# A tuned FFT-and-MoE kernel: six transfers are asked for by GpSimd in place of SyncE

## The chip, the cores and the metric

The kernel runs on one core of a Trainium2 chip. The metric is the device time of one execution in microseconds (us), median of several runs. TensorE (PE in the profile; PEld is its weight load), VectorE (DVE), ScalarE (ACT), GpSimd (POOL) and SyncE (SP) each work through their own list of instructions in order. SP computes nothing here: it only asks for transfers. A transfer asked for by SP or by GpSimd is then carried by the same 16 DMA engines; the profile calls the queue of SP's transfers q1 and that of GpSimd's q0.

## The reference

`x` has 8 batches of 3008 rows of 256 numbers. A real FFT over the rows, a complex 256 x 256 product with a soft threshold of 0.01, and the inverse FFT give `y`; then a two-layer network with an ELU between its layers runs on all 24064 rows.

```python
X = np.fft.rfft(x, axis=1)
Yr = Xr @ w_r - Xi @ w_i + b_r
Yi = Xr @ w_i + Xi @ w_r + b_i
Yr = np.sign(Yr) * np.maximum(np.abs(Yr) - lam, 0.0)   # Yi alike
y = np.fft.irfft(Y, n=x.shape[1], axis=1)
h = y @ w_in
g = np.where(h > 0.0, h, np.exp(np.minimum(h, 0.0)) - 1.0)
out = g @ w_out
```

## The kernel before

**The network's loop.** The rows of all batches are cut into 47 blocks of 512. Each block takes 8 iterations of the main loop (L1313), one for each pair of 128-wide slices of the hidden layer: `front` multiplies into `hps` (L1115) and ScalarE takes the exponential, `elu` and `finish_elu` finish the ELU on GpSimd or VectorE, and two iterations later `back` adds the pair to the block's output sums `ps_o` (L1189). After its 8th pair a block is copied to `osb`, one half by VectorE and one by ScalarE (L1200), and stored by four transfers of 128 rows each (L1209); some of these are cut in two where they cross a stretch of the output. `osb` has two buffers, so a block's copies need the stores of the block two before it to have ended.

**The FFT's units.** Both transforms are done as matrix products in two stages, cut into small units. While the network works on one batch, units of the next are put between its iterations by hand: `plan` writes, for each of a batch's 47 iterations, which units go ahead of the network's products (`f0`) and which after them (`f1`). For batch 1 they stand in the list `mid` (L1224) from iteration 10 on. A unit X is the second stage of the forward transform. Units M multiply by the weights and apply the threshold on GpSimd (L314, L315), six pairs q = 0 to 5, each into a tile `Y`. Units B are the first stage of the inverse, one for each pair. Units Y (`n` in `mid` for batch 1) are the second stage and give `yT`, which `front` reads. Units A belong to the forward transform of batch 2.

**The path around the change.** When the second half of pair q is done, `turn_Y` (L433) lets SP move `Y` to `Yx` with the parts re-ordered: `by_part` (L424) issues four transfers of 64 KB, for s = 0 with c = 0 and c = 1, then for s = 1 with c = 0 and c = 1 (L428). c chooses the half of the 128 partitions that is written. Unit B(1, q) then multiplies (L448): two products for s = 0, which need both c of s = 0, and two for s = 1. Its result is copied to `Bz`, by ScalarE alone (L150) or, for q = 5, half by ScalarE (L456) and half by VectorE (L457), and for q = 2 to 5 each quarter of `Bz`'s 256 KB goes to the DRAM tile `DB` in a transfer of its own (L466). `load_Bs` (L479) reads `DB` back in another order as `Bs`; the first of four such loads is cut, for batch 1, into 80 rows that come from pairs 0 to 4 and 16 rows that come from pair 5. The first unit Y of batch 1, Y(1, 0), reads that first `Bs` (L612), and the network needs its `yT` from iteration 40 on, where block 5 crosses from batch 0 to batch 1.

**What SP's list holds there.** Output block 3 (rows 1536 to 2047 of batch 0) ends in iteration 33. So SP's list runs in this order: four `Yx` transfers of pair 5; the `DB` store of pair 3; the four stores of block 3; the `DB` stores of pairs 4 and 5; the two parts of the first `Bs`; a store of batch 2's `DA` (L221); the other three `Bs`. SP takes them strictly one after another, and each waits for its own data first. GpSimd's list holds, at the same place, the threshold of pair 5 and then the ELU's minimum (L1166) of much later iterations, since between them the ELU is finished on VectorE.

Of the kernel before, what the change touches and what calls it, by code (L numbers as in the profile page):

```python
# [20 lines left out]
N2 = 64  # L21
# [8 lines left out]
def kernel(  # L30
# [11 lines left out]
    nc = tc.nc  # L42
    P = nc.NUM_PARTITIONS

    B, S, D = x.shape
# [375 lines left out]
        for Y_, yb, ch in todo:  # L421
            nc.vector.scalar_tensor_tensor(Y_, yb, LAM, ch, ALU.add, ALU.min)

    def by_part(dst, of):  # L424

        for s in range(2):
            for c in range(2):
                nc.sync.dma_start(dst[c * N2 : c * N2 + N2, :, s, :], of(c, s))  # L428

    def turn_M3():  # L430
        by_part(M3x, lambda c, s: M3[c][s * N2 : s * N2 + N2])

    def turn_Y(b, q):  # L433
        Y = Y_of.pop((b, q))
        Yx_of[b, q] = Yx = wk4.tile([P, 2, 2, D], BF16, name="Yx", tag="Y")
        by_part(Yx, lambda c, s: Y[s * N2 : s * N2 + N2, :, c * D : c * D + D])

    def unit_B(b, v, alone=False, on_dve=False, all_dve=False):
        if (b, v // 2) not in Bz_of:
# [643 lines left out]
    def pieces(t, k):  # L1083

        out_, c = [], 0
        while c < k:
            b, r = divmod(t + c, S)
            e = min(k, c + S - r)
            out_.append((b, r, c, e))
            c = e  # L1090
        return out_
# [79 lines left out]
    def back(i, split):  # L1171
        blk, fp = divmod(i, NPAIR)
        bs = blk * TB
        gT = g_of.pop(i)
        nq = TB // P // 2
        if fp == 0:
            po_of[blk] = [
                psO.tile([P, 2, E], F32, name="ps_o", tag="outp") for _ in range(nq)
            ]
        po = po_of[blk]  # L1180
        last = i == n - 1
        order = [(q, s, j) for q in range(nq) for s in range(2) for j in range(2)]
        if i == 0:
            order.sort(key=lambda z: z[1])
        elif last:
            order.sort(key=lambda z: (z[0], z[2]))
        for q, s, j in order:
            ft, i_ = 2 * fp + s, 2 * q + j
            nc.tensor.matmul(  # L1189
                po[q][:, j, :], lhsT=gT[:, s, i_ * P : i_ * P + P],  # L1190
                rhs=w_out_r[:, ft, :], start=(ft == 0 and j == 0),
                stop=(ft == NFT - 1), skip_group_check=True,
            )
        if fp < NPAIR - 1:
            return
        osb = late2.tile([P, 4, E], F32, name="osb", tag="osb")
        for q in range(nq):
            copy = nc.vector.tensor_copy if (last and q) or (split and q == 0) else nc.scalar.copy
            if not (last and q):
                copy(osb[:, 2 * q : 2 * q + 2, :], po[q][:])  # L1200
            for i_ in range(2 * q, 2 * q + 2):
                if last and q:
                    copy(osb[:, i_, :], po[q][:, i_ % 2, :])
                for b, t, c0, c1 in pieces(bs + i_ * P, P):
                    ov = out[b * S : b * S + S, :].rearrange("(r w j) e -> w r j e", w=4, j=8)
                    while c0 < c1:
                        w, r0 = t // WT, t % WT // 8
                        k = min(c1 - c0, (w + 1) * WT - t)
                        (nc.scalar if last and i_ % 2 else nc.sync).dma_start(  # L1209
                            ov[w, r0 : r0 + k // 8], osb[c0 : c0 + k, i_, :]  # L1210
                        )
                        t, c0 = t + k, c0 + k
        del po_of[blk]
# [4 lines left out]
    def plan(b):  # L1218
# [38 lines left out]
        for t, u in enumerate(seq, lead):  # L1257
            if u is None:
                continue
            if b and n1 < B:  # L1260
                mode[t] = "act" if u in on_act or u[0] == "M" else "pool"
            if mode[t] == "act" and u[0] != "M":
                k = {"y": "Y"}.get(u[0], u[0])
                c = {"y": b, "A": n2}.get(u[0], n1)
                if c < B:
                    dve = (False, True) if k == "B" else (k != "X" or b < 3 and u[1] == 7,)
                    f0[t].append(put(k, c, u[1], False, *dve))
            elif u[0] == "y":
                f0[t].append(put("Y", b, u[1]))
            elif u[0] == "n":  # L1270
                f0[t].append(put("Y", n1, u[1]))
            elif u[0] == "A":
                if n2 < B:
                    f0[t].append(put("A", n2, u[1]))
            elif b == 0 and u == ("B", 5):
                f0[t].append(put("B", n1, 5, False, True))
            else:
                f0[t].append(put(u[0], n1, *u[1:]))
            if u[0] == "M" and u[2] == 1:
                f1[t].append((turn_Y, (n1, u[1])))  # L1280
            if u == ("B", 5):
                for w, k in enumerate((0, 2, 3, 4)):
                    f1[t + k].append((load_Bs, (n1, w, 0, 4 * K1 - 16 * (b == w == 0))))
            if u == ("A", 5) and n2 < B:
                for part in ((0, 8), (8, NS)):
                    f1[t] += [(load_Z, (n2, a, *part)) for a in range(3)]
# [26 lines left out]
    for i in range(n + LAG):  # L1313
        if i == FILL:
            few.close()
        if i == LAG:
            back(0, False)
# [21 lines left out]
        if i < n:  # L1339
            for f, a in f1[r]:  # L1340
                f(*a)
            split = i > LAG and (i - LAG) % NPAIR == NPAIR - 1
            if split:
                back(i - LAG, True)
            elu(i, *h, pooled, on_act)
            if PER <= i < PER + 4:
                three_weights(*divmod(i - PER, 2))
            if 1 <= i < 5:
                if i < 3:
                    scale_w_in(2, True, i - 1)  # L1350
                scale_w_in(3, False, (i - 1) // 2, (i - 1) % 2)
            if i == n - 2:
                early_h = front(n - 1, True, False)
            elif early_h:
                early_h = None
        else:
            split = False
        if i > LAG and not split:
            back(i - LAG, False)
# [30 lines left out]
```

## Time and profile before

| | us |
|---|---|
| median of 3 runs | 873.0 |
| lowest and highest of them | 871.7, 874.85 |
| the profiled execution: time on the device | 873.84 |
| its span in the trace | 872.1 |
| TensorE matmul busy (share of the span) | 861.3 (99%) |
| ScalarE busy | 715.2 (82%) |
| VectorE busy | 665.9 (76%) |
| GpSimd busy | 589.4 (68%) |

The span is the time from the first to the last instruction of the trace; 1.7 us of the profiled execution lie around it. Busy times do not count the asking for transfers. In a timeline row the first two numbers are the start and the duration in us, then come the engine (SPq is SP's queue), the line, the operation, what it writes and reads, how many were merged (x4), and in brackets the engine's idle time just before and what ended it.

### The profile page before, as it was taken

The numbers are of one execution on the slowest core, as the hardware profiler recorded it, in microseconds if no ns is written. First come the engines' busy times: TensorE is split into PE (matmuls) and PEld (weight loads), VectorE is DVE, ScalarE is ACT, GpSimd is POOL, SyncE is SP. The second block draws the span as 40 slices with busy tenths as digits, with TensorE's granted clock in tenths as the row PEclk, the third lists the DMA queues.
The fourth block names the chain that finished last, engine by engine and source line by source line (L and its number), as shares of the span: only waits on it lengthen the run. The fifth ranks groups of instructions, "written<-read, shape, count | busy, mean of one in ns | idle before, by whom it ended". The sixth has DMA issues, their size and how long they took to land.

```text
span 872.1 us, 18551 instructions
## 1 busy us (share of the span) xinstructions
PE 861.3 (99%) x6773; PEld 675.6 (77%) x6773; DVE 665.9 (76%) x1103; ACT 715.2 (82%) x1255; POOL 589.4 (68%) x860
## 2 busy tenths in 40 slices
PE   8999999999999999999999999999999999999997
PEld 6567677887788877877778887788777878787776
DVE  8889778697776876768866787777777687788775
ACT  7878888888978889798887988879887888876664
POOL 8671630898757986588856888459874697734664
PEclk9999999999999999999999999999999999999999
DMA  8796446542484225653365342653337313240111
GB/s 248 263 300 208 115 114 196 161 142 73 122 242 140 80 73 157 208 159 96 87 179 182 123 110 74 210 159 116 97 92 221 88 38 86 76 144 25 40 36 49
DMA packets 114205, 116.11 MB, mean 133 GB/s; under 512 B 11569, under 2 KB 104241, under 8 KB 110753
## 3 DMA queue, kind: packets, MB, share of 16 engines
q1 hardware_dynamic: 109376, 87.40, 35.2%
q0 software_dynamic: 4448, 27.26, 9.4%
q8 instruction: 53, 0.87, 0.4%
q14 instruction: 40, 0.32, 0.1%
q10 hardware_dynamic: 288, 0.26, 0.1%
HBM read 53.28 MB, written 48.23 MB: 116 GB/s over the span
## 4 chain that ended last, share of the span: by engine, by line
PE 94%; DMA 2%; DVE 1%; POOL 1%; ACT 1%; issue 1%; SPq 0%; DVEq 0%; POOLq 0%
PE ps_o L1189 39%; PE hps L1115 34%; PE mps L334 6%; PE xps L242 3%; PE yps L612 2%; PE mps L1115 2%; PE bps L448 2%; PE aps L194 2%; PE mps L292 2%; DMA xt<-in_x_dram 1%; DMA yb<-in_w_i_dram 0%; DMA Bs<-DB 0%; DMA DB<-Bz 0%; DVE gT L1156 0%; PE aps L186 0%
## 5 line engine op out<-in xcount | busy, mean ns | idle before, releaser
L1156 DVE SCALAR_TENSOR_TENSOR gT<-Et,hps 128x512 fp32r<-128x512 f32 x630 | 402.8, 682 | 137.3 <-POOL Et L1166 127.3
L1189 PE MATMUL ps_o<-w_out_r,gT 128*128 128x256 f32 x3008 | 477.3, 301 | 0.0
L1189 PEld LDWEIGHTS ps_o<-w_out_r,gT 128*128 128x128 f32 x3008 | 404.3, 189 | 48.0 <-DVE osb L1200 0.2
L1166 POOL TENSOR_SCALAR Et<-Et 128x512 f32<-128x512 f32 x482 | 287.4, 615 | 208.2 <-ACT Et L1127 206.7
L1115 PE MATMUL hps<-yT,w_in_s 128*128 128x512 bf16 (+7 forms) x1620 | 366.7, 353 | 0.3
L1127 ACT ACTIVATE Et<-hps 128x512 f32<-128x512 f32 x514 | 282.7, 609 | 41.7 <-PE hps L1115 38.6
L1115 PEld LDWEIGHTS <-w_in_s 128*128 128x128 bf16 x1728 | 144.1, 98 | 104.8 <-issue 13.2
L1125 ACT ACTIVATE Et<-hps 128x512 f32<-128x512 f32 x192 | 104.5, 597 | 42.0 <-PE hps L1115 41.6
L1130 ACT ACTIVATE Et<-Et 128x512 f32<-128x512 f32 x192 | 110.5, 632 | 0.0
L350 POOL TENSOR_TENSOR Y<-yb,clip 128x512 bf16<-128x512 f32 x72 | 92.7, 1287 | 6.0
L346 POOL TENSOR_TENSOR yb<-yb,bias_bc 128x256 f32<-128x256 f32 x72 | 53.2, 739 | 11.3 <-DVE yb L341 11.2
L150 ACT CAST XT<-xps 128x768 bf16<-128x768 f32 x57 | 45.8, 804 | 15.9 <-PE xps L242 15.7
L150 ACT CAST yT<-yps 128x752 bf16<-128x752 f32 x56 | 44.1, 787 | 14.4 <-PE yps L612 14.4
L341 DVE TENSOR_TENSOR yb<-mps,yb 128x512 f32<-128x512 f32 x72 | 49.8, 692 | 7.2
L1158 DVE SCALAR_TENSOR_TENSOR gT<-hps,Et 128x512 fp32r<-128x512 f32 x78 | 50.2, 685 | 3.3
L349 POOL TENSOR_SCALAR clip<-yb 128x512 f32<-128x512 f32 x72 | 44.1, 613 | 6.3
L150 ACT CAST A<-aps 128x1024 bf16<-128x1024 f32 x40 | 40.7, 1019 | 7.9 <-PE aps L194 4.9
L150 ACT CAST Bz<-bps 128x1024 bf16<-128x1024 f32 x41 | 41.6, 1014 | 5.3 <-PE bps L448 5.0
L340 DVE TENSOR_TENSOR yb<-mps,bias_bc 128x256 f32<-128x256 f32 x72 | 30.5, 423 | 17.5 <-PE mps L334 15.7
L334 PE MATMUL mps<-wcat_s,XT 128*128 128x256 bf16 x288 | 43.2, 273 | 0.0
L1200 DVE COPY osb<-ps_o 128x512 f32<-128x512 f32 x46 | 31.7, 689 | 5.4 <-PE ps_o L1189 3.4
L260 POOL TENSOR_TENSOR XS<-XT 128x512 bf16<-128x512 bf16 x30 | 34.1, 1157 | 2.4 <-ACT XT L150 1.4
(214 smaller groups left out, 670.1 us busy)
## 6 DMA issues: line engine op xcount, KB each, us to landing
xt<-in_x_dram POOLq DMA_DIRECT2D x21, 1024.0 KB, 5.5
out_dram<-osb SPq DMA_DIRECT2D x158, 128.0 KB
Bs<-DB SPq DMA_DIRECT2D x30, 384.0 KB
Yx<-Y SPq DMA_DIRECT2D x168, 64.0 KB
DA<-A SPq DMA_DIRECT2D x19, 512.0 KB
DB<-Bz SPq DMA_DIRECT2D x19, 512.0 KB
Z<-DA SPq DMA_DIRECT2D x21, 384.0 KB
xt<-in_x_dram POOLq DMA_DIRECT2D x6, 512.0 KB, 5.8
```

Of the source, the lines that this page charges most:

```text
L150: nc.scalar.copy(dst, src)
L334: nc.tensor.matmul(out_, lhsT=lhs[:, dt] if lhs is not None else sum_of(dt, ch)[:, oc : oc + P], rhs=w[:, dt, :], start=(dt == 0), stop=(d ...
L346: nc.gpsimd.tensor_tensor(yb[:, D : 2 * D], yb[:, D : 2 * D], bias_bc[:, D : 2 * D], ALU.add)
L350: nc.gpsimd.tensor_tensor(Y_of[b, q][:, i, :], yb[:], clip[:], ALU.subtract)
L1115: nc.tensor.matmul(hps[s][:, c0:c1], lhsT=w_in_s[:, dt, ft * P : ft * P + P], rhs=yT_of[b][:, dt, t0 : t0 + c1 - c0], start=(dt == 0), sto ...
L1125: nc.scalar.activation(Et[:, s], hps[s], AF.Relu, scale=-1.0)
L1127: nc.scalar.activation(Et[:, s], hps[s], AF.Exp)
L1130: nc.scalar.activation(Et[:, s], Et[:, s], AF.Exp, scale=-1.0)
L1156: nc.vector.scalar_tensor_tensor(o, e, -1.0, h, ALU.add, ALU.max)
L1158: nc.vector.scalar_tensor_tensor(o, h, 0.0, e, ALU.max, ALU.add)
L1166: nc.gpsimd.tensor_scalar(e, e, 1.0, 0.0, ALU.min, ALU.max)
L1189: nc.tensor.matmul(po[q][:, j, :], lhsT=gT[:, s, i_ * P : i_ * P + P], rhs=w_out_r[:, ft, :], start=(ft == 0 and j == 0), stop=(ft == NFT ...
```

## The change

In `turn_Y` of batch 1's last pair, q = 5, the transfers with c = 1 (for s = 0 and for s = 1) are issued by GpSimd and those with c = 0 by SP as before. The four stores of output block 3 are issued by GpSimd. Nothing else differs: PE, DVE and ACT have the same instructions in the same order. SP's list loses six transfers and keeps the order of the others. In GpSimd's list the six stand behind the last threshold of pair 5 and ahead of the next minimum of the ELU: the two `Yx` pieces, then the four stores.

```diff
-    def by_part(dst, of):
+    def by_part(dst, of, shared=False):
 
         for s in range(2):
             for c in range(2):
-                nc.sync.dma_start(dst[c * N2 : c * N2 + N2, :, s, :], of(c, s))
+                eng = nc.gpsimd if shared and c else nc.sync
+                eng.dma_start(dst[c * N2 : c * N2 + N2, :, s, :], of(c, s))
...
-        by_part(Yx, lambda c, s: Y[s * N2 : s * N2 + N2, :, c * D : c * D + D])
+        by_part(
+            Yx, lambda c, s: Y[s * N2 : s * N2 + N2, :, c * D : c * D + D], (b, q) == (1, 5)
+        )
...
-                        (nc.scalar if last and i_ % 2 else nc.sync).dma_start(
+                        eng = nc.scalar if last and i_ % 2 else nc.sync
+                        (nc.gpsimd if blk == 3 else eng).dma_start(
                             ov[w, r0 : r0 + k // 8], osb[c0 : c0 + k, i_, :]
                         )
```

## The prediction

> **What bounds the kernel now.** I read the page's busy times first, then the chain of work that ended last, then what TensorE waited for.
>
> ```profile
> span 872.1 us, 18551 instructions
> PE 861.3 (99%) x6773; PEld 675.6 (77%) x6773; DVE 665.9 (76%) x1103; ACT 715.2 (82%) x1255; POOL 589.4 (68%) x860
> PE 94%; DMA 2%; DVE 1%; POOL 1%; ACT 1%; issue 1%; SPq 0%; DVEq 0%; POOLq 0%
> ```
>
> TensorE is busy in 861.3 of 872.1 us and carries 94% of the chain. So the change, which takes no instruction from TensorE, can gain only what TensorE stands idle for a transfer. The list of TensorE's waits has two such rows behind the start-up:
>
> ```profile
> PE yps L612 <- DMA Bs<-DB: 0.5, 1, 0.5
> PE bps L448 <- DMA Yx<-Y: 0.4, 1, 0.4
> ```
>
> Each is one wait (the columns are us in total, times, longest). Both have a count of one in a span of eight batches, so they belong to one place each; TensorE's timeline shows where.
>
> ```profile
> 128.41 0.39 PE L448 MATMUL bps<-Yx,M3x 128*128 128x256 bf16 x2
> 129.22 0.39 PE L448 MATMUL bps<-Yx,M3x 128*128 128x256 bf16 x2 [0.41 <-DMA Yx<-Y]
> 138.76 0.49 PE L612 MATMUL yps<-M,Bs 96*128 96x94 bf16 x8 [0.52 <-DMA Bs<-DB]
> ```
>
> The first is unit B(1, 5): its two products for s = 0 run at 128.41 without a wait, those for s = 1 could start at 129.22 - 0.41 = 128.81 and stand 0.41 us for the last `Yx` piece. The second is Y(1, 0), which stands 0.52 us for its `Bs`. Together 0.93 us, 0.11% of the span. That is the ceiling.
>
> **Part one, the two `Yx` pieces.** SP's timeline gives the issues, the chain in order of time gives the landing.
>
> ```profile
> 125.15 2.54 SPq L428 DMA_DIRECT2D Yx<-Y  x4
> 127.74 0.59 SPq L466 DMA_DIRECT2D DB<-Bz  x1
> 128.38 3.84 SPq L1209 DMA_DIRECT2D out_dram<-osb  x4
> 132.32 1.15 SPq L466 DMA_DIRECT2D DB<-Bz  x2
> 127.09 2.09 DMA Yx<-Y
> ```
>
> Four issues take 2.54 us, 0.64 each; the fourth starts at about 127.09 and its data is there 2.09 us later, at 129.18. What is late is the issue, not the data: the tile `Y` was ready at 125.12 (GpSimd's row below, 123.84 + 1.28). With the change SP issues s = 0 at 125.15 and s = 1 at 125.79, which lands at 125.79 + 2.09 = 127.88 and is no longer late. GpSimd issues its two from 125.15 as well.
>
> ```profile
> 123.84 1.28 POOL L315 TENSOR_TENSOR Y<-yb,clip 128x512 bf16<-128x512 f32 x1
> 151.68 1.19 POOL L1166 TENSOR_SCALAR Et<-Et 128x512 f32<-128x512 f32 x2 [26.55 <-ACT Et L1127]
> 70.92 1.26 POOL L121 DMA_DIRECT2D xt<-in_x_dram  x2
> ```
>
> GpSimd's own price is hidden: an issue takes 0.63 us there (1.26 for two), six take 3.8 us, and GpSimd stands idle for 26.55 us at that place. Without that idle time the 3.8 us would push the ELU's minimum, which VectorE and then TensorE wait for. Its second piece is issued at 125.15 + 0.63 = 125.78. How long it then takes to land is the one cost that no row shows: GpSimd issues no transfer as small as 64 KB in this trace. The nearest rows are its loads of `x`, 512 KB to 1 MB each:
>
> ```profile
> L121 POOL DMA_DIRECT2D xt<-in_x_dram x27: 575/597/887, 1.2 to 593.6; - x27
> DMA to landing us min/median/max: 4.1/5.5/9.7
> 371.78 0.59 POOL L121 DMA_DIRECT2D xt<-in_x_dram  x1
> DMA to landing us min/median/max: 5.2/5.2/5.2
> DMA  0000000009923556979989999897721006994588
> ```
>
> The last row is the DMA share in 40 slices of 371.5 to 378 us, 0.1625 us each, with one load of 1 MB issued at 371.78, whose landing took the 5.2 us of the row before it. Nothing moves until the tenth slice, 371.5 + 9 x 0.1625 = 372.96, so the first bytes come 1.18 us after the issue began; the busy stretch ends with the 31st slice, at 376.54, and lasts 3.58 us. For 1/16 of the bytes the move would be 0.22 us. The tail to the landing is 371.78 + 5.2 - 376.54 = 0.44. So 64 KB come to an estimate of 1.18 + 0.22 + 0.44 = 1.84 us, next to the 2.09 us of SP's row. I bound the landing by 1.4 us (head and move with no tail) and by the loads' longest, 9.7 us, and take 2.1, nearest to SP's row, which has the same bytes: the piece lands at 127.88, with 0.93 us to spare before 128.81. The s = 0 piece lands 0.63 us sooner, at 127.25, ahead of 128.41. So the wait of 0.41 us goes: **-0.41**.
>
> A rule of the Trainium skill speaks against this: "DMA: Bandwidth & Descriptors", section "Issuing engine by pattern", gives plain loads and stores to SyncE as the generally faster issuer, and its specifications put the first byte at about 1 us from GpSimd against 0.6. By these the piece would be some 0.4 us later, and the sum the same, since that fits in the margin.
>
> **Part two, the four stores.** In the SP rows above they keep the queue from 128.38 to 132.3, 3.84 us, and behind them stand the `DB` stores of pairs 4 and 5. When their data were ready:
>
> ```profile
> 127.06 1.06 ACT L150 CAST Bz<-bps 128x1024 bf16<-128x1024 f32 x1
> 130.27 0.69 DVE L457 CAST Bz<-bps 128x512 bf16<-128x512 f32 x1 [0.43 <-ACT Bz L456]
> 132.95 2.82 DMA DB<-Bz
> 135.79 2.83 DMA Bs<-DB
> 138.62 0.14 issue
> ```
>
> Pair 4 was ready at 128.12, pair 5 at 130.96, but SP reached them at 132.32 and 132.95. From there it is one string: 2.82 us until `DB` has landed, the load of the 16 rows at 135.79, 2.83 us until `Bs` is there, Y(1, 0) at 138.76. After the change SP's list is: `Yx` to 126.4, the `DB` store of pair 3 to 127.0, of pair 4 at 128.1, of pair 5 when its data come, 130.96 - 0.41 = 130.55. It lands at 130.55 + 2.82 = 133.4, the 16 rows at 133.4 + 2.83 = 136.2. TensorE could take Y(1, 0) at 138.76 - 0.52 = 138.24, and 0.41 earlier after part one, at 137.83. So 1.6 us are to spare, and the second wait goes too: **-0.52**. If part one gains nothing, `DB` 5 goes out at 130.96 and the margin is 1.6 still, so part two doesn't hang on part one. What is late next is nothing on TensorE: its list of waits has no further transfer behind this place.
>
> The stores themselves: their `osb` halves are ready at 126.56 (VectorE) and 127.21 (ScalarE), as the rows here show, and GpSimd reaches them at 126.4. They are all issued by about 129.2 rather than 132.2. Nobody waits for their landing before block 5's copies, from 161.99 on.
>
> ```profile
> 125.87 0.69 DVE L1200 COPY osb<-ps_o 128x512 f32<-128x512 f32 x1 [0.23 <-PE ps_o L1189]
> 126.59 0.62 ACT L1200 COPY osb<-ps_o 128x512 f32<-128x512 f32 x1
> 161.99 0.68 DVE L1200 COPY osb<-ps_o 128x512 f32<-128x512 f32 x1
> ```
>
> Their 512 KB now move from about 127.8, while `DB` 3 does; the `Yx` pieces stand ahead of them in GpSimd's queue, and the margins of 0.93 and 1.6 us are there for what they lose to that. That contention I take as 0, with the margins as its bound.
>
> **The sum.** -0.41 - 0.52 = -0.93: span 871.2, the profiled execution 873.84 - 0.93 = 872.9. The median of the runs shown, 873.0, is 0.84 below the profiled execution, so the median goes to **872.1**. A measurement of this kernel can tell about 0.3%, 2.6 us, from no change; the ceiling of 0.93 lies well inside that.
>
> **The rivals.**
>
> *GpSimd's pieces land late (slower).* In their place, B(1, 5), TensorE runs in order, so a late piece stops everything. The wait taken out is replaced by (125.78 + landing) - 128.81. With the second wait gone, the kernel is slower from a wait above 0.93 us, a landing above 3.96 us; every load in the trace is above that, but those carry 8 to 16 times the bytes. At the shortest load's 4.1 us the wait would be 1.07, the net +0.1: 873.1. At the median 5.5 it would be 2.47, net +1.5: 874.5. Slower by over 2.6 us needs a landing above 6.6 us; at 9.7 the wait is 6.67 and the net +5.7, 878.7. For it: the load that was issued at 88.97 among other transfers took 8.7 us. Against it: the quiet load's first bytes came after 1.18 us, and the rest was moving 1 MB.
>
> ```profile
> 88.97 0.59 POOL L121 DMA_DIRECT2D xt<-in_x_dram  x1
> DMA to landing us min/median/max: 8.7/8.7/8.7
> ...
> 127.00:128.00 1.00, 1.00 (x8) 0.83 (x7) 0.97 (x2) 1.00 (x3) 0.00 (x0) 1.00 0.47 116
> 128.00:129.00 1.00, 0.81 (x7) 0.48 (x6) 0.78 (x2) 1.00 (x3) 0.00 (x0) 1.00 0.44 107
> ```
>
> The DMA share around B(1, 5) is 0.47 and 0.44 (the last two rows, the number before the GB/s), so there is room.
>
> *Only the second wait goes.* VectorE could hold up GpSimd's piece. Its minimum at 126.76 takes 1024 elements in the time of 512 elsewhere (0.68 us for L1156, 128x512), so it runs at double rate:
>
> ```profile
> 126.76 0.69 DVE L1168 TENSOR_SCALAR Et<-Et 128x1024 f32<-128x1024 f32 x1 [0.20 <-ACT Et L1127]
> 163.22 0.68 DVE L1156 SCALAR_TENSOR_TENSOR gT<-Et,hps 128x512 fp32r<-128x512 f32 x1
> ```
>
> If the piece's first bytes, due at 125.78 + 1.18 = 126.96, were held until 127.45 by it, the landing would move by 0.5 to 0.7 us, to 128.6 at most, still inside the margin; with contention of another 0.6 us or more the wait of 0.41 stays, and the net is -0.52: 872.5. The Trainium skill, "SBUF — State Buffer", section "SBUF: two separate sides", states such a lock: while VectorE runs an operation in its two-port mode, GpSimd can't write the descriptors of its transfers. No run here shows one stalled by it.
>
> *The change is given back or does nothing.* ScalarE could become the limit in 126 to 131 us, where it is busy for the whole of both slices above (ACT is the fourth engine of the row). Against it: it stood 0.54 us for B(1, 5) itself (ScalarE's row below) and more behind, so it follows TensorE's earlier start. Net 0: 873.0.
>
> ```profile
> 129.65 0.58 ACT L456 CAST Bz<-bps 128x512 bf16<-128x512 f32 x1 [0.54 <-PE bps L448]
> ```
>
> **How the numbers follow.** Both waits gone, 872.1: 0.70. Only the second, 872.5: 0.14. Given back, 873.0: 0.08. Late pieces, 873.1 to 878.7: 0.08, of which 0.03 above 2.6 us. The runs before lie 1.3 below and 1.85 above their median. The range is 870.5 to 874.3: 872.1 less 1.6, the mean of the two spreads, at the low end, 872.5 with 1.85 at the high end, which takes in late pieces up to a landing of about 5 us. Spread alone could carry a result over the 2.6 us to either side: 0.04 for faster, 0.02 for slower. So faster 0.04, slower 0.05, same 0.91.
>
> **What would show it.** Right: TensorE's list of waits has neither row; GpSimd shows two `Yx` and four `osb` issues from 125.1 to about 129.2, SP the `DB` stores near 126.4, 128.1 and 130.6 and the first `Bs` loads near 131.2 and 133.4. Wrong: an idle time before B(1, 5) that names `Yx` and is above 0.41, and then how long a GpSimd transfer of 64 KB takes; or an idle time before Y(1, 0) with `DB` 5 issued on time, which would put the delay in the data's movement; or all rows as forecast and TensorE's idle time found at some other place.

## The result and the profile after

The changed kernel takes 871.25 us (median of 22 runs, 870.79 to 873.71), the kernel before in the same comparison 872.6 (22 runs, 871.39 to 874.85). The ratio is 0.9987 with a 95% interval of 0.9981 to 0.9993, so 1.1 us less, between 0.6 and 1.7 (the two medians differ by 1.35). With 22 runs of each the interval is much narrower than the 2.6 us that the prediction took for the limit of what can be told, so the gain is clear of noise. The prediction was -0.93 from 873.0, to 872.1.

The page of the changed kernel, to be laid beside the rows of before:

```profile
span 869.3 us, 18553 instructions
PE 860.8 (99%) x6773; PEld 675.8 (78%) x6773; DVE 666.2 (77%) x1103; ACT 715.4 (82%) x1255; POOL 592.8 (68%) x866
q1 hardware_dynamic: 108512, 86.74, 35.2%
q0 software_dynamic: 4704, 27.92, 9.8%
```

The span is 2.8 us shorter, more than 1.1 us, so one profiled execution must not be read as the result. TensorE's timeline splits it. These are the first products of B(1, 4), then those of B(1, 5), Y(1, 0) and Y(1, 1), after:

```profile
124.77 0.61 PE L451 MATMUL bps<-Yx,M3x 128*128 128x256 bf16 x4
127.04 0.61 PE L451 MATMUL bps<-Yx,M3x 128*128 128x256 bf16 x4
...
136.18 0.51 PE L615 MATMUL yps<-M,Bs 96*128 96x94 bf16 x8
138.33 0.51 PE L615 MATMUL yps<-M,Bs 96*128 96x94 bf16 x8
```

and before (the rows of B(1, 5) and Y(1, 0) stand in the prediction):

```profile
126.15 0.61 PE L448 MATMUL bps<-Yx,M3x 128*128 128x256 bf16 x4
...
140.91 0.51 PE L612 MATMUL yps<-M,Bs 96*128 96x94 bf16 x8
```

Up to B(1, 4) the changed kernel is 1.38 us ahead, at a point that the change has not reached: that is start-up, which differs from one execution to the next. From B(1, 4) to Y(1, 1) it takes 13.56 us against 14.76, that is **1.20 us less at the place of the change**. From there to the end of the span it is 731.0 against 731.2. So 1.20 is the change's share, and it agrees with the ratio of the runs. This stretch, B(1, 4) to Y(1, 1), is called the local measure below, since start-up doesn't reach it.

Both waits are gone: the rows of B(1, 5) and Y(1, 0) have no bracket, and B(1, 5) is one row of four products instead of two rows of two. The queues show the new order. GpSimd's timeline and the landings of its pieces:

```profile
122.46 1.28 POOL L315 TENSOR_TENSOR Y<-yb,clip 128x512 bf16<-128x512 f32 x1
124.04 1.29 POOL L429 DMA_DIRECT2D Yx<-Y  x2 [0.30 <-POOL Y L315]
125.48 2.29 POOL L1213 DMA_DIRECT2D out_dram<-osb  x4 [0.16 <-issue]
149.09 1.20 POOL L1169 TENSOR_SCALAR Et<-Et 128x512 f32<-128x512 f32 x2 [21.32 <-ACT Et L1130]
...
DMA to landing us min/median/max: 2.4/2.5/2.5
```

SP's timeline:

```profile
123.77 1.24 SPq L429 DMA_DIRECT2D Yx<-Y  x2
125.10 4.34 SPq L469 DMA_DIRECT2D DB<-Bz  x3
130.11 3.23 SPq L482 DMA_DIRECT2D Bs<-DB  x2
```

The six GpSimd issues end at 127.77, and GpSimd still stands idle for 21.32 us behind them. SP gives out the `DB` stores as their data come (one transfer of 256 KB for each pair), without stores of block 3 between them.

### The profile page after: what moved, and what is told of

Same layout as the page of the kernel before. It is cut to its first block, busy times and chain, and to the rows that moved or that the text cites. A ratio compares the mean times of both kernels' runs of the same rounds, so it can differ in the third digit from the quotient of the medians.

```text
span 869.3 us, 18553 instructions
## 1 busy us (share of the span) xinstructions
PE 860.8 (99%) x6773; PEld 675.8 (78%) x6773; DVE 666.2 (77%) x1103; ACT 715.4 (82%) x1255; POOL 592.8 (68%) x866
## 3 DMA queue, kind: packets, MB, share of 16 engines
q1 hardware_dynamic: 108512, 86.74, 35.2%
q0 software_dynamic: 4704, 27.92, 9.8%
## 4 chain that ended last, share of the span: by engine, by line
PE 94%; POOL 2%; DVE 1%; DMA 1%; ACT 1%; issue 0%; DVEq 0%; POOLq 0%
PE ps_o L1192 39%; PE hps L1118 34%; PE mps L334 5%; PE xps L242 3%; PE mps L1118 2%; PE yps L615 2%; PE bps L451 2%; PE mps L292 2%; PE aps L194 2%; POOL Y L350 1%; DMA xt<-in_x_dram 1%; PE aps L186 0%; POOL yb L346 0%; POOL clip L349 0%; DVE gT L1159 0%
## 5 line engine op out<-in xcount | busy, mean ns | idle before, releaser
L150 ACT CAST XT<-xps 128x768 bf16<-128x768 f32 x57 | 45.8, 804 | 14.1 <-PE xps L242 13.9
```

The source lines that it names most:

```text
L150: nc.scalar.copy(dst, src)
```

## The experiments

The theory, called the issue theory: both waits came from the time at which SP's queue reached an issue, and whatever brings those issues forward takes them away. Rivals: GpSimd's way of carrying data is what helps; the stores must leave SP; GpSimd's issues are free anyway. All experiments start from the kernel before or the changed one, and each was timed beside runs of the kernel before. The waits are those that TensorE's list names at this place.

| kernel | local, us | named waits of TensorE | median, us (before) | ratio, 95% interval |
|---|---|---|---|---|
| before | 14.76 | 0.41 + 0.52 | | |
| changed | 13.56 | none | 871.25 (872.6) | 0.9987, 0.9981 to 0.9993 |
| e1 pieces only | 13.57 | none | 871.59 (872.57) | 0.9993, 0.9984 to 1.0002 |
| e2 stores only | 14.40 | 0.73 | 872.01 (872.57) | 0.9994, 0.9986 to 1.0003 |
| e3 stores later on SP | 14.10 | 0.41 | 872.14 (872.57) | 0.9996, 0.9987 to 1.0005 |
| e4 all four pieces | 14.96 | 0.80 + 0.32 | 872.87 (872.57) | 1.0005, 0.9996 to 1.0014 |
| e5 one issue ahead | 14.37 | 0.68 | 871.96 (872.5) | 0.9998, 0.9989 to 1.0007 |
| e7 on ScalarE | 15.31 | 1.50 + 1.34 | 874.69 (872.5) | 1.0027, 1.0017 to 1.0037 |
| e8 pieces, stores later | 13.59 | none | 872.18 (872.5) | 0.9993, 0.9984 to 1.0002 |
| e10 one ahead, stores later | 14.38 | 0.71 | 872.88 (871.88) | 1.0007, 0.9998 to 1.0016 |

The waits of e7 are for ScalarE, the others for transfers; its local measure begins behind its first wait of 1.50. e6 and e9 change the later batches and stand further below. Between kernels a fraction of a microsecond apart the local measure decides; the intervals of the times are 0.5 to 0.9 us to each side, and most of them overlap.

**e1, the pieces without the stores.** The changed kernel with block 3's stores on SP again:

```diff
-                        (nc.gpsimd if blk == 3 else eng).dma_start(
+                        eng.dma_start(
```

> Only the two Yx pieces with c = 1 go to GpSimd; block 3's four stores stay on SP. Local measure: from the start of B(1,4)'s products to the start of Y(1,1)'s products on TensorE, 14.76 us before (126.15 to 140.91) and 13.56 after (124.77 to 138.33). Issue theory (what counts is when SP's queue reaches an issue): the wait of B(1,5) goes, and SP reaches the DB store of pair 5 two issues, 1.28 us, sooner than before, while TensorE comes about 0.5 us sooner, so Y(1,0)'s wait of 0.52 shrinks to nothing or nearly: local 13.6 to 13.9, time 0.7 to 1.2 us under before. Rival (the stores must leave SP for the second wait to go): Y(1,0) still waits 0.5 us or more, local 14.2 or above, time 0.4 to 0.6 under before.

SP's timeline in e1:

```profile
123.67 1.25 SPq L429 DMA_DIRECT2D Yx<-Y  x2
125.00 0.55 SPq L469 DMA_DIRECT2D DB<-Bz  x1
125.60 2.52 SPq L1213 DMA_DIRECT2D out_dram<-osb  x4
128.22 1.64 SPq L469 DMA_DIRECT2D DB<-Bz  x2
```

The local measure is 13.57, that of the changed kernel. With two issues less and the four stores in 2.52 us instead of 3.84, SP reaches pair 4's `DB` store at 128.22 and pair 5's at 129.0, just as its data come. (The 3.84 us of before are not four equal issues: three took 0.54 to 0.61 us and the fourth 1.92. What held that one up is not shown.) So the two pieces alone bring the whole gain, and the rival, that the stores must leave SP, falls.

**e2, the stores without the pieces**: `turn_Y` never shares.

```diff
-            Yx, lambda c, s: Y[s * N2 : s * N2 + N2, :, c * D : c * D + D], (b, q) == (1, 5)
+            Yx, lambda c, s: Y[s * N2 : s * N2 + N2, :, c * D : c * D + D], False
```

> Only block 3's four stores go to GpSimd; all four Yx pieces stay on SP. Issue theory: B(1,5) keeps its wait of about 0.41 for the fourth piece, Y(1,0)'s wait of 0.52 goes: local measure (14.76 before, 13.56 after) 14.0 to 14.2, time 0.5 to 0.7 under before. Rival (the way the data are carried, not the queue: GpSimd's six transfers show as 256 packets where SP's showed 864): both waits shrink, since the stores are what was made lighter, local 13.6.

B(1, 5) on TensorE and the last piece in the chain, e2:

```profile
128.28 0.39 PE L451 MATMUL bps<-Yx,M3x 128*128 128x256 bf16 x2 [0.73 <-DMA Yx<-Y]
...
125.83 2.40 DMA Yx<-Y
```

Y(1, 0) no longer waits, B(1, 5) does, as expected, but for 0.73 us where 0.41 was expected: the fourth piece takes 2.40 us to land, against 2.09 before and in e3, where the stores come later. The local measure is 14.40 and not 14.0 to 14.2. Moving the stores alone has a price: they now run beside the pieces.

**e3, everything on SP, the stores later.** The kernel before; block 3's stores are noted and issued by SP in iteration 35, behind the first two parts of `Bs`:

```diff
+                        if blk == 3:
+                            put_off.append((to, of))
...
+            if i == 35:
+                for to, of in put_off:
+                    nc.sync.dma_start(to, of)
```

> Nothing goes to GpSimd: all transfers stay on SP, but block 3's four stores stand in its list behind the two parts of the first Bs instead of ahead of the DB stores of pairs 4 and 5. Issue theory: like the stores alone on GpSimd, Y(1,0)'s wait goes, B(1,5)'s wait of 0.41 stays: local 14.0 to 14.2, time 0.5 to 0.7 under before. Rival (GpSimd's way of carrying is what helps): no change against before, local 14.7.

TensorE in e3, B(1, 5) and Y(1, 0):

```profile
129.04 0.39 PE L448 MATMUL bps<-Yx,M3x 128*128 128x256 bf16 x2 [0.41 <-DMA Yx<-Y]
...
137.91 0.51 PE L612 MATMUL yps<-M,Bs 96*128 96x94 bf16 x8
```

The wait of Y(1, 0) goes without GpSimd doing anything; 14.10 is as the issue theory had it. GpSimd's way of carrying is not the cause. e3 also prices each wait by itself: the second is worth 14.76 - 14.10 = 0.66 (named with 0.52), the first 14.10 - 13.56 = 0.54 (named with 0.41).

**e4, all four pieces on GpSimd.** From the changed kernel:

```diff
-                eng = nc.gpsimd if shared and c else nc.sync
+                eng = nc.gpsimd if shared else nc.sync
```

> All four Yx pieces of pair 5 and the four stores go to GpSimd. Issue theory: four issues in one queue again, so the fourth piece starts 0.30 + 3 x 0.65 = 2.25 us after Y is ready and lands 2.4 later, at 4.65, against 1.97 + 2.09 = 4.06 on SP: B(1,5) waits about 1.0 us (0.41 before), Y(1,0) does not wait: local 14.4 to 14.7, time within 0.4 of before. Rival (carriage by GpSimd helps in itself): B(1,5) waits no longer than before, local 14.1 or less.

GpSimd's and TensorE's rows in e4:

```profile
123.80 2.75 POOL L429 DMA_DIRECT2D Yx<-Y  x4 [0.29 <-POOL Y L315]
...
127.76 0.39 PE L451 MATMUL bps<-Yx,M3x 128*128 128x256 bf16 x2 [0.80 <-DMA Yx<-Y]
128.48 0.39 PE L451 MATMUL bps<-Yx,M3x 128*128 128x256 bf16 x2 [0.32 <-DMA Yx<-Y]
```

Four issues take 2.75 us here and 2.54 on SP, so one queue is as slow as the other, and B(1, 5) waits 1.12 in two parts. The local measure is 14.96, a little above the 14.4 to 14.7 expected, since the pieces for s = 0 came late as well: the first three take 2.9, 3.2 and 2.9 us to land. GpSimd is no better carrier; for these pieces two queues are what helps.

**e5 and e10, the margin.** The changed kernel (e5), and e8 below (e10), with one transfer of 32 KB more ahead of GpSimd's pieces, into a tile that nobody reads:

```diff
+        if shared:
+            nc.gpsimd.dma_start(space[:], idm[:])
         for s in range(2):
             for c in range(2):
                 eng = nc.gpsimd if shared and c else nc.sync
```

> The changed kernel with one small transfer more (32 KB, 128 rows of 256 B, into a tile that nobody reads), which GpSimd issues just ahead of its two Yx pieces, so that these are issued about 0.65 us later. Margin as the changed kernel's trace has it (second piece issued 0.97 us after Y is ready and landed 2.4 later, at 127.1, where TensorE comes to it at 127.26): the 0.65 exceeds the margin by 0.5, B(1,5) waits 0.4 to 0.6 us for Yx, local measure (13.56 in the changed kernel) 14.0 to 14.3, time 0.4 to 0.7 above the changed kernel. Rival, the margin of 0.93 that the prediction gave: no wait, local 13.6.

> The extra 32 KB transfer ahead of GpSimd's two pieces again, but block 3's stores on SP behind the first Bs loads. With the stores on GpSimd right behind, the second piece landed 3.15 us after its issue against 2.4. If the stores' traffic made that, it lands in 2.4 here and B(1,5) waits 0 to 0.2 us. If the small transfer ahead of it in GpSimd's own queue made it (128 rows of 256 B), it lands in about 3.1 again and B(1,5) waits 0.5 to 0.7.

The second piece in the chain of e5, with its wait:

```profile
125.05 3.15 DMA Yx<-Y
...
128.24 0.38 PE L453 MATMUL bps<-Yx,M3x 128*128 128x256 bf16 x2 [0.68 <-DMA Yx<-Y]
```

and of e10:

```profile
125.79 3.20 DMA Yx<-Y
...
129.03 0.38 PE L453 MATMUL bps<-Yx,M3x 128*128 128x256 bf16 x2 [0.71 <-DMA Yx<-Y]
```

The wait is a little above what e5 expected (0.68 us for 0.4 to 0.6, local 14.37 for 14.0 to 14.3), and the way was another. The extra issue delays the second piece by only 0.2 us (1.17 after `Y` is ready in e5, where the changed kernel has 0.97), because it fills the 0.30 us in which GpSimd waited for `Y`. But the piece then takes 3.15 us to land instead of 2.4. e10 shows that block 3's stores aren't needed for that: with the stores far away it takes 3.20 all the same (2.3 in e8, which has no extra transfer). It isn't simply that a transfer stands ahead in the queue either, since the first piece, directly behind the extra one, lands in 2.3 us in both. SP's `DB` store of pair 3 moves at that time. The first issue of these rows is that store, in e5, e10 and e4:

```profile
125.24 5.11 SPq L471 DMA_DIRECT2D DB<-Bz  x3
...
126.00 5.14 SPq L471 DMA_DIRECT2D DB<-Bz  x3
...
124.16 6.44 SPq L469 DMA_DIRECT2D DB<-Bz  x3
```

In e5 and e10 the second piece is issued 0.2 us ahead of that store (125.05 and 125.79), in the changed kernel and e8, where it lands in 2.3 to 2.4 us, 0.4 ahead. In e4 the store comes among the four pieces, and three of them take 2.9 us or more with no extra transfer. VectorE's minimum, which the prediction feared, overlaps the end of the piece's issue by 0.13 us in e5 and e10; but in e6 such a minimum overlaps an issue of batch 1 by 0.24 (issued at 102.58), and the piece lands in 2.2 us. So the traffic of SP's store fits best; no run takes it away, and this cause is not shown. In sum the piece is about 1 us later, for a wait of 0.7: the margin was small, not the 0.93 of the prediction.

**e7, the six issues on ScalarE.** From the changed kernel, `nc.scalar` in place of `nc.gpsimd` at both places:

```diff
-                eng = nc.gpsimd if shared and c else nc.sync
+                eng = nc.scalar if shared and c else nc.sync
...
-                        (nc.gpsimd if blk == 3 else eng).dma_start(
+                        (nc.scalar if blk == 3 else eng).dma_start(
```

> ScalarE issues the six transfers instead of GpSimd; they stand in ScalarE's list where they come in the program. Issue theory with cover: sharing the issues takes the waits for transfers away on any second queue, but ScalarE has no idle time there (share 1.00 in 126 to 129 us); six issues of about 0.65 and the wait for Y put 3 to 4 us into its list, of which two iterations of lag and its small gaps hide part: TensorE waits for ScalarE, local measure 14.3 to 17, time 0.7 to 3 us above the changed kernel. Rival (a second queue is all that matters): local 13.6, time as the changed kernel.

ScalarE's timeline, and TensorE's, in e7:

```profile
123.77 1.53 ACTq L429 DMA_DIRECT2D Yx<-Y  x2
125.34 1.01 ACT L150 CAST Bz<-bps 128x1024 bf16<-128x1024 f32 x1 [1.89 <-PE ps_o L1192]
...
126.41 0.60 PE L451 MATMUL bps<-Yx,M3x 128*128 128x256 bf16 x4 [1.50 <-ACT Bz L150]
130.16 0.60 PE L451 MATMUL bps<-Yx,M3x 128*128 128x256 bf16 x4 [1.34 <-ACT Bz L150]
```

It is 2.2 us slower than before and 3.4 slower than the changed kernel, a little more than the 0.7 to 3 expected. ScalarE stands with its two issues until `Y` is ready and until they are out; behind them in its list is the copy of B(1, 3), 125.34 instead of 123.36 in the changed kernel, and the next unit B can't have its PSUM bank before that. No lag of two iterations lies between the two. A second queue is not enough, it needs idle time at that place.

**e8, the pieces shared and the stores later on SP**: the edit of e3 and the shared pieces of the changed kernel.

> The two pieces with c = 1 on GpSimd, and block 3's stores on SP behind the two parts of the first Bs. Issue theory: both waits of TensorE are gone, as in the changed kernel; local 13.5 to 13.6, time within 0.4 of it. Contention (stores beside the DB stores make these land late: 3.9 us for pair 5 in the changed kernel, 2.82 before): here pair 5's DB store lands in 2.5 to 3.0 us again. If the stores' traffic does not matter, it lands in 3.5 or more here too.

The local measure is 13.59, the changed kernel's. The contention shows in how long pair 5's `DB` store takes to land, read from when SP can issue the 16 rows that wait for it. In the changed kernel, two rows of SP's instructions in a narrow window (duration in ns min/median/max, then first and last start):

```profile
L469 SPq DMA_DIRECT2D DB<-Bz x1: 360/360/360, 129.1 to 129.1; - x1
...
L482 SPq DMA_DIRECT2D Bs<-DB x1: 319/319/319, 133.0 to 133.0; - x1
```

and in e8:

```profile
L469 SPq DMA_DIRECT2D DB<-Bz x1: 359/359/359, 131.7 to 131.7; - x1
...
L482 SPq DMA_DIRECT2D Bs<-DB x1: 319/319/319, 134.1 to 134.1; - x1
```

3.9 us with the stores beside it, 2.4 without (e2 has 4.1, e3 2.4). So in the changed kernel the stores on GpSimd use up margin that e8 keeps, 1.5 us of it, and neither reaches TensorE. It is not the stores' bytes alone. In e1 the same stores go out at the same time, from 125.6 on, but by SP, ahead of this `DB` store in one queue, and it lands in 3.1 us although its own issue takes 0.89:

```profile
L469 SPq DMA_DIRECT2D DB<-Bz x1: 887/887/887, 129.0 to 129.0; - x1
...
L482 SPq DMA_DIRECT2D Bs<-DB x1: 320/320/320, 132.1 to 132.1; - x1
```

What makes the stores dearer beside it in GpSimd's queue than ahead of it in SP's was not tested. The times of e8 and the changed kernel can't be told apart.

**e6 and e9, the cover.** GpSimd issues the two pieces of every pair of every batch (e6: `True` in place of `(b, q) == (1, 5)`), or of each batch's last pair (e9: `q == 5`).

> GpSimd issues the two pieces with c = 1 for every pair of every batch, not for one: 84 issues of about 0.65 us in place of 2, 53 us more on GpSimd, most of it where GpSimd is busy with the threshold and the ELU's minimum. Cover theory: GpSimd's idle time hid the issues at pair (1,5); here an issue holds up the minimum behind it by up to 1.3 us, VectorE waits longer for GpSimd (135 us before), and TensorE has two iterations, about 4 us, of slack, so part of it comes through: time 0.5 to 4 us above the changed kernel. Rival (TensorE is so far the limit that GpSimd's issues cost nothing anywhere): within 0.4 us of the changed kernel. Rival (SP's queue held up other pairs too): below the changed kernel by 0.4 us or more.

> GpSimd issues the two pieces with c = 1 of the last pair (q = 5) of every batch, so of six pairs more than in the changed kernel; with all 36 pairs of the later batches the time rose 44.6 us, 1.24 per pair. By count (each GpSimd issue in the later batches passes straight through): 6 x 1.24 = 7.4 us above the changed kernel. By place (what matters is whether GpSimd has idle time behind it before its debt reaches TensorE): behind the last pair of batch 2 the changed kernel's GpSimd stands 0.86 to 1.08 us idle in each following iteration, so a debt of 1.55 us is paid back in two, within the two iterations of lag: 0 to 1.5 us above the changed kernel, and no waits of TensorE for gT in its list.

e6 takes 917.2 us (before 872.5), ratio 1.0513, 1.0499 to 1.0527; e9 876.34 (before 871.88), ratio 1.0046, 1.0032 to 1.0059. Both expectations missed. GpSimd's timeline of e6 in batch 2:

```profile
180.52 1.29 POOL L350 TENSOR_TENSOR Y<-yb,clip 128x512 bf16<-128x512 f32 x1
181.76 0.75 POOL L346 TENSOR_TENSOR yb<-yb,bias_bc 128x256 f32<-128x256 f32 x1
182.60 0.61 POOL L349 TENSOR_SCALAR clip<-yb 128x512 f32<-128x512 f32 x1
183.30 1.29 POOL L350 TENSOR_TENSOR Y<-yb,clip 128x512 bf16<-128x512 f32 x1
184.88 1.26 POOL L429 DMA_DIRECT2D Yx<-Y  x2 [0.29 <-POOL Y L350]
186.17 0.75 POOL L346 TENSOR_TENSOR yb<-yb,bias_bc 128x256 f32<-128x256 f32 x1
```

and what TensorE waits for there:

```profile
PE hps L1118 <- DVE gT L1159: 26.2, 25, 2.6
```

In the later batches' threshold phase GpSimd works without a gap. Each pair adds 0.29 of waiting for its own `Y` and 1.26 of issues, 1.55 us. e6 is 44.7 us above before and so 45.8 above the changed kernel; in batch 1 it keeps pace with that (local 13.57), so all of it falls on the 36 pairs of the later batches, 1.27 each. The list names 26.2 us of it; most of the rest is longer busy time of TensorE, 878.4 us against 860.8. The lag of two iterations that was to absorb it is used up by then. In e9, where GpSimd has gaps behind the last pair, the ratio gives 4.0 us above before and so 5.1 above the changed kernel for six pairs: fewer than by count (7.4), more than by place (0 to 1.5). The traces tell where: from B(b, 4) to B(b, 5) e9 takes 0.51 to 0.57 us longer than the changed kernel in batches 2 to 6 and 1.22 longer in batch 7, 3.9 us in all. In batch 2 it is one row of TensorE:

```profile
230.16 1.19 PE L1118 MATMUL hps<-yT,w_in_s 128*128 128x512 bf16 x4 [0.20 <-DVE gT L1159]
```

Only 0.20 us is named, but from the products ahead of this row to those behind it e9 takes 1.67 us (229.33 to 231.00), the changed kernel 1.15 (226.92 to 228.07): 0.52 lost. Between the 3.9 us of the traces and the 5.1 of the ratios 1.2 us stay open; the interval of e9's ratio alone is 1.2 us to each side.

## Why the prediction was right

- **What bounds the kernel, and the two places**: right. TensorE's two waits for transfers were all that there was to gain, though at 1.20 us and not 0.93, and nothing else moved: behind Y(1, 1) both kernels take 731 us.
- **Part one**: the wait is gone, for the reason given, that the fourth issue was late and not its data (e4 puts it back with four issues in the other queue). Three numbers of the step were off in one direction. GpSimd starts 0.30 us after `Y` is ready (SP 0.03), and its 64 KB land in 2.4 to 2.5 us against the 2.1 taken. The second piece was there at 124.71 + 2.4 = 127.1, and TensorE came for it at about 127.26 (the third of the four products in the row at 127.04): 0.15 us to spare, where 0.93 was forecast. Third, TensorE comes sooner than taken, 3.52 us after `Y` is ready and not 3.69: the named idle time from which 128.81 was worked out is itself too short. The bounds held it; that these 0.15 us were left was luck as much as working.
- **The rule that GpSimd's transfers start later**: the Trainium skill's 0.4 us ("DMA: Bandwidth & Descriptors", Specifications), which is for the first byte, is the size of what the landing shows, 2.4 to 2.5 against SP's 2.09. The first bytes differ less here: in the changed kernel GpSimd's first packet starts 1.35 us after its issue began, SP's 1.25. "That fits in the margin" held by the same 0.15.
- **Part two**: the wait of Y(1, 0) is gone, but the step that gave it to the four stores was not needed: e1 loses it with the pieces alone. I had counted the stores' issues at 3.84 us, the row of before, as if they took that long anywhere; behind two issues fewer they took 2.52. The claim that part two doesn't hang on part one holds (e2 and e3).
- **"That contention I take as 0"**: this term failed. The stores beside the `DB` store made it land in 3.9 us, not 2.82 (2.4 in e8), and in e2 the fourth piece in 2.40, not 2.09. Of the margin of 1.6 us that ate 1.1, and the price stayed hidden. In part one the pieces gave no sign of the stores: the second landed in 2.4 us with them on GpSimd and with them on SP (e1).
- **The sum**: -0.93 was an undercount; the local measure gives -1.20, the ratio of the runs -1.1. In each kernel with waits named at this place the loss is their sum and 0.11 to 0.15 us for each (e3: 0.54 for 0.41; e4: 1.40 for 1.12 in two; the first of e7: 1.65 for 1.50). The idle time named for the products leaves out what a break costs in the pipeline: two rows of 0.39 take 0.78 where one row of four takes 0.61. The weight loads' idle time, 0.69 for each wait, is the other side; the cost lies between the two.
- **The late pieces (the slower rival)**: not here, but near, as e5 shows: a landing 0.75 us longer brings the wait back.
- **VectorE holding GpSimd up**: the pieces were issued by 125.33, ahead of VectorE's double-rate minimum at 125.39. The first store, issued at 125.48 beside it, took 0.71 us against 0.53 to 0.54 for the others. e4 shifts GpSimd's issues against that minimum, and the long issue goes with it: there the first store takes 0.58, but the third piece, issued beside the minimum, 0.88 (0.60 to 0.67 for the other pieces), and the third store, beside the next one at 127.53, 0.70. From e4:

```profile
L429 POOL DMA_DIRECT2D Yx<-Y x1: 879/879/879, 125.1 to 125.1; - x1
...
125.15 0.69 DVE L1171 TENSOR_SCALAR Et<-Et 128x1024 f32<-128x1024 f32 x1 [0.20 <-ACT Et L1130]
```

  That fits the lock that the Trainium skill states ("SBUF — State Buffer", "SBUF: two separate sides"). So this rival stood close: the pieces' issues ended 0.06 us ahead of the minimum.
- **GpSimd's price, hidden by its idle time**: right at this place; e6 is the price without cover.

## What to carry to other kernels

When the last of several issues in one queue is what a bound engine waits for, dividing them between two queues takes the wait away, and it suffices to move those; reordering a queue can do the same without a second engine. The second queue must belong to an engine that is idle there: the same two issues per pair were free at one place and cost 1.27 us per pair at others. Count a wait of TensorE as more than its named idle time (0.11 to 0.15 us more at this place, 0.3 in e9), and when a transfer is called hidden, give the margin by its worst neighbour, not by its quiet time.

## What the runs showed of the hardware

- **GpSimd's transfers go in larger packets.** Six transfers left SP's q1 with 864 packets less (109376 to 108512) and came to q0 with 256 more (4448 to 4704). The size counts of the two pages show 768 packets fewer under 2 KB and 160 more from 2 to 8 KB; 160 packets for 640 KB are 4 KB each. Their landing was no quicker for it.
- **The same 64 KB take 2.3 to 3.2 us to land by GpSimd's queue**: 2.3 to 2.4 in e8, 3.15 and 3.20 in e5 and e10, 2.5 to 3.2 in e4. SP's `DB` store of 256 KB, moving at the same time, fits as the cause and was not tested.
- **TensorE's clock fell after waits of over 2 us.** In e6 it stood for 2.12 us before 194.69; the stretches behind (TensorE's clock is the number ahead of the last two):

```profile
194.00:195.00 1.00, 0.31 (x2) 0.19 (x2) 1.00 (x2) 0.00 (x0) 1.00 (x2) 1.00 0.40 84
195.00:196.00 1.00, 0.99 (x5) 0.44 (x3) 0.90 (x3) 0.60 (x1) 1.00 (x2) 0.63 0.00 0
196.00:197.00 1.00, 1.00 (x6) 0.91 (x6) 1.00 (x3) 0.66 (x2) 0.91 (x2) 0.50 0.00 0
```

  The clock stays at half for about 3.4 us in all. The Trainium skill ("TensorE: Matmul & The Clock Gate", Part 1) has the half clock come after an idle window of about 3.4 us; here a shorter stand was enough. In e6 the clock fell behind all three waits of over 2 us (2.12, 2.09 and 2.63) and behind none of the others, up to 1.44; nor did it behind the 1.50 of e7. The same fall came in start-up in the profiled executions of e8 and e9 (0.50 and 0.66 in 24 to 28 us in e8), and not in those of before or changed. An estimate from these rows: 3.4 us at half the clock lose up to 1.7 us. So the fall can be part of why times of one kernel spread over some 3 us, more than the whole effect studied here; the profiled executions of e8 and e9 were the slowest of their runs.
